# Two routing tables instead of four, filled by rows of 9,248 bytes, and the low half of w_out made by TensorE instead of GpSimd

## The chip, the core and the metric

The kernel runs on one core of a Trainium2 chip. The metric is the device time of one execution in microseconds, as a median over runs. The profile names the engines PE (TensorE, with PEld for its weight loads), DVE (VectorE), ACT (ScalarE), POOL (GpSimd) and SP (SyncE, which issues most DMAs; SPq and POOLq are the two issuing queues).

## What is computed

Eight batches of 576 tokens go through an attention with 32 packed keys (`_attn_ref`), a dense layer with a gate (`_moe_ref`), and a top-1 mixture of eight experts (`_moe2_ref`). Cut to what matters here:

```python
p_packed = sm_attn(p, k, v); out = sm_attn(q, p_packed, p_packed)   # 8 batches, 8 heads, 576 tokens, 64 wide
x = out as [4608, 512]
h = x @ w_in; g = h * sigmoid(h); x = g @ w_out                      # w_in [512, 2048], w_out [2048, 512]
e_idx = argmax(x @ w_gate)                                           # one of 8 experts per token
out[t] = gate[t] * eom[t] * (relu(x[t] @ w1[e]) @ w2[e])
```

## The kernel before

Everything is float32. TensorE multiplies at full rate in the rounded format float32r, so each factor is split into a high half (the value rounded to float32r) and a low half (value less high half), and each product is made of three matmuls: low by high, high by low, high by high.

The weights `w_in` and `w_out` come as 64-bit floats. `f64_load` (L432) brings a piece into a staging buffer, and `f64_conv` turns it into float32 on DVE with three instructions (L452, L455, L458). A piece of `w_in` goes straight into the tile `w_in`. A piece of `w_out` (128x512, 16 of them) goes into a tile `wf` (two buffers), and `split_out` then makes its two halves: `wo[0]`, the high one, by a cast on ACT (L469), and `wo[1]`, the low one, by a subtraction on POOL (L470).

All this happens while the first batch runs. A batch is a loop over 16 steps f. In a step PE makes `mm1(f)` (12 matmuls, L664) into the one buffer `ps_h`; ACT (L673) and DVE (L674) make `g` of it; ACT and DVE split it into `ghi` (L679) and `glo` (L684), and the 64 columns left over into `gl` (L691, and L693 on POOL in batch 0); PE makes `mm2(f-2)` (12 matmuls, L715). `mm1(f+1)` needs `ps_h` free, which is when `g(f)` is done. Into this loop are laid, by hand, the pieces of the attention of the next batch (`s1` to `s9`) and the products `step_m`. In batch 0 two or three pieces of the weights are converted in each step as well: one between `mm1` and `g`, one after `glo`. PE's small products share one PSUM buffer, the tag `a` (two of the eight banks; the others are the four accumulators and `ps_h`).

After step 4 of batch 0, `setup_late` fills the routing tables. Each token's place in its expert's list is found batch by batch; `place` (L782) scatters the token numbers into tables in DRAM by indirect DMAs from POOL. Block i goes to table i modulo NPERM (L35), so that scatters to one table, which have to wait for one another, stand four apart. Every slot must hold a default beforehand; the table that got no token adds nothing, and the sum over the tables is the token's row. `fetch_ix` reads the tables (L910, one DMA for each) and adds them up on POOL (L911, L912). The experts then run one block of 128 tokens after another.

The order on each engine is the order of the code. A DMA issued from SP waits in SP's queue until its buffer is free, and everything behind it waits too.

Of the kernel before, what the change touches and what calls it, by code (L numbers as in the profile page):

```python
# [8 lines left out]
F32 = mybir.dt.float32  # L9
F32R = mybir.dt.float32r  # L10
BF16 = mybir.dt.bfloat16
U32 = mybir.dt.uint32
I32 = mybir.dt.int32
ALU = mybir.AluOpType
AF = mybir.ActivationFunctionType
# [9 lines left out]
E8 = 8  # L25
F2 = 1024
NTOK = B * S
NBLK = NTOK // 128
CAP = NBLK
NPAIR = NBLK + E8 - 1  # L30
XW = DM + 1
# [3 lines left out]
HS = S // 2  # L35
EARLY = 3
NSTATIC = NBLK + 2
NPERM = 4
PW = 16


def constants():
    p = np.arange(128)
    c = np.zeros((128, C_END), np.float32)
    c[:, C_ID:C_ID + 128] = np.eye(128)
    e = np.arange(E8)
    c[:, C_E:C_E + E8] = e
    c[:, C_OFF:C_OFF + E8] = (e - E8) * CAP
    c[:, C_LT:C_LT + E8 * E8] = (e[None, :] < e[:, None]).reshape(1, -1)
    c[:, C_J] = p  # L50
    k = np.full((128, 256), 0x3F80, np.uint16)
    k[:, :128] *= p[:, None] < p[None, :]
    t = np.stack([block_tokens(i) for i in range(NBLK)], axis=1).astype(np.int32)
    t[:, np.arange(NBLK) % NPERM > 0] -= NTOK
    t = np.concatenate([t, np.zeros((128, PW - 1), np.int32)], axis=1)
    return {"cst": c, "cstk": k, "cstt": t}

# [17 lines left out]
def run(steps):  # L75
    now = list(steps)
    steps.clear()
    for st in now:
        st()


class Kernel:
    def __init__(self, tc, ins, out):
# [3 lines left out]
        self.ws2 = nc.dram_tensor("ws2", (E8, 4, 2, 128, 2 * DM), F32, kind="Internal").ap()  # L87
        self.perm = [nc.dram_tensor(f"perm{i}", ((E8 * CAP + 1) * 128, PW), I32, kind="Internal").ap() for i in range(NPERM)]
        self.xr = nc.dram_tensor("xr", (NTOK + 1, XW), F32, kind="Internal").ap()
# [5 lines left out]
    def run(self):  # L95
        tc, nc = self.tc, self.nc
# [20 lines left out]

        self.flip = False
        self.ppt, self.m, self.g, self.loads = {}, {}, {}, {}
        self.graws = []  # L120
        self.wgt = cp.tile([128, 4, E8], F32, name="wgt")
        self.tok = self.rt.tile([128, NBLK + PW - 1], I32, name="tok")
        self.w_in = self.pin.tile([128, 4, FF], F32, name="w_in")
# [42 lines left out]
    def setup_late(self):  # L166
        nc = self.nc
        nc.sync.dma_start(self.tri, self.i["cstk"].bitcast(BF16).rearrange("p (a b) -> p a b", a=2))
        nc.sync.dma_start(self.tok, self.i["cstt"])
        nc.gpsimd.memset(self.nt_run, 0.0)  # L170
        for i, perm in enumerate(self.perm):
            if i < 2:
                fill = self.stg.tile([128, E8 * CAP + 1], I32, tag="wf", bufs=2, name="fill")
                nc.gpsimd.memset(fill, 0 if i else NTOK)
            nc.sync.dma_start(perm.rearrange("(p c) w -> p (c w)", p=128).rearrange("p (w c) -> p w c", w=PW),
                              fill.unsqueeze(1).to_broadcast([128, PW, E8 * CAP + 1]))
        z = self.rt.tile([128, 5, XW], F32, tag="xr", name="zrow")[:1, 0]
        nc.gpsimd.memset(z, 0.0)
        nc.sync.dma_start(self.xr[NTOK:NTOK + 1, :], z)

    def pick(self):
        assert self.group is None and not self.late
# [90 lines left out]
    def prologue(self):  # L273
        nc = self.nc
# [55 lines left out]
        m_lo()  # L330
        att["s8", 1]()
        self.warm(24)
        att["s9", 0]()
        att["s9", 1]()
        self.gl = [self.p1.tile([128, NF, 128], F32R, tag=f"gl{i}", name="gl") for i in range(2)]

    def batch(self, b, hook=None):
        sched = self.extra_steps(b)
        for f in range(NF):
            s = b * NF + f  # L340
# [15 lines left out]
            self.fill(b, 2 if f < 2 else 1)  # L356
            if s > 1:
                self.mm2(*divmod(s - 2, NF))
            if slot and f == 1:
                self.split_slot()  # L360
            if wait and f == 1:
# [9 lines left out]
            if b == 0 and f == 0:  # L371
                t = self.rt.tile([128, 4, 512, 2], U32, tag="wg", name="stg4")
                for i in range(4):
                    self.f64_load(t[:, i], True)
            if b == 0 and f == 14:
                self.mid = self.rt.tile([128, E8 * DM], F32, tag="wg", name="mid")
                self.nc.sync.dma_start(self.wgt, self.i["wgt"])
            if b == 0 and f == 15:
# [88 lines left out]

    def split_out(self, w, f):
        self.nc.scalar.copy(out=self.wo[0][:, f, :], in_=w)  # L469
        self.nc.gpsimd.tensor_tensor(out=self.wo[1][:, f, :], in0=w, in1=self.wo[0][:, f, :].bitcast(F32), op=ALU.subtract)  # L470


    def split_store(self):
# [425 lines left out]
    def fetch_ix(self, j):  # L899
        nc = self.nc  # L900
        if j < EARLY:
            off = nc.values_load(self.ptab[0:1, 1 + j:2 + j], engines=[ENG.SP], min_val=0, max_val=E8 * CAP * 128)
            self.ex[j] = self.estar
        else:
            off = nc.values_load(self.tab[0:1, 0, j:j + 1], engines=[ENG.SP], min_val=0, max_val=E8 * CAP * 128)
            self.ex[j] = nc.values_load(self.tab[0:1, 1, j:j + 1], engines=[ENG.SP], min_val=0, max_val=E8 - 1)
        ix = self.rt.tile([128, NPERM + 2], I32, tag="xix_p", bufs=4, name="xix_p")
        at = self.rt.tile([128, 1], I32, tag="xix", bufs=6, name="xix")
        for i, perm in enumerate(self.perm):
            nc.sync.dma_start(ix[:, i:i + 1], perm[bass.ds(off, 128), 0:1])  # L910
        nc.gpsimd.tensor_tensor(out=ix[:, 4:6], in0=ix[:, 0:2], in1=ix[:, 2:4], op=ALU.add)  # L911
        nc.gpsimd.tensor_tensor(out=at, in0=ix[:, 4:5], in1=ix[:, 5:6], op=ALU.add)  # L912
        return at.bitcast(U32)

    def flag(self, j):
# [134 lines left out]
```

## Time and profile before

| | |
|---|---|
| time, median of 3 runs | 1361.1 us (1360.93 to 1362.29) |
| the profiled execution: its time, its span | 1360.51 us, 1358.7 us |
| PE busy | 1269.3 us, 93% |
| DVE, ACT, POOL busy | 653.9, 505.8, 173.4 us |
| batch 0: first and last `g` (L674) | 31.99 and 178.95 us |
| granted TensorE clock, mean | 0.971 of full speed |

The profile is of one execution. Times are counted from the start of its span. A busy PE is one whose matmuls are in flight; how fast they go depends on the granted clock, which has two levels, 1.2 GHz (shown as 0.50) and 2.4 GHz (1.00).

### The profile page before, as it was taken

The numbers are of one execution on the slowest core, as the hardware profiler recorded it, in microseconds if no ns is written. First come the engines' busy times: TensorE is split into PE (matmuls) and PEld (weight loads), VectorE is DVE, ScalarE is ACT, GpSimd is POOL, SyncE is SP. The second block draws the span as 40 slices with busy tenths as digits, with TensorE's granted clock in tenths as the row PEclk, the third lists the DMA queues.
The fourth block names the chain that finished last, engine by engine and source line by source line (L and its number), as shares of the span: only waits on it lengthen the run. The fifth ranks groups of instructions, "written<-read, shape, count | busy, mean of one in ns | idle before, by whom it ended". The sixth has DMA issues, their size and how long they took to land. (4 is left out here: it accounts for less than half of the span.)

```text
span 1358.7 us, 24463 instructions
## 1 busy us (share of the span) xinstructions
PE 1269.3 (93%) x8414; PEld 1020.1 (75%) x8416; DVE 653.9 (48%) x1417; ACT 505.8 (37%) x980; POOL 173.4 (13%) x236
## 2 busy tenths in 40 slices
PE   7754699999999899999999999999999999999997
PEld 3543578778788688787787788878888888888886
DVE  6953965845865745857556745232222222222221
ACT  3321255445464444454454433223223222222322
POOL 0220310100010100101000111112212212211210
PEclk9686899999999999999999999999999999999999
DMA  7598346846695855776665414442557383722630
GB/s 292 205 233 210 110 151 222 274 158 223 211 292 180 257 197 189 227 285 209 225 219 193 104 32 157 108 127 71 193 173 249 121 301 97 277 66 69 236 129 23
DMA packets 118303, 247.72 MB, mean 182 GB/s; under 512 B 30177, under 2 KB 56609, under 8 KB 118178
## 3 DMA queue, kind: packets, MB, share of 16 engines
q1 hardware_dynamic: 110946, 226.35, 51.0%
q0 software_dynamic: 7232, 19.72, 4.4%
q8 instruction: 77, 1.26, 0.4%
q14 instruction: 48, 0.39, 0.1%
HBM read 401.92 MB, written 96.29 MB: 367 GB/s over the span
## 5 line engine op out<-in xcount | busy, mean ns | idle before, releaser
L715 PE MATMUL acc<-wo,ghi 128*128 128x512 f32 x1024 | 320.9, 395 | 0.0
L715 PEld LDWEIGHTS acc<-wo,ghi 128*128 128x128 f32 x1024 | 194.5, 190 | 39.0
L664 PE MATMUL ps_h<-a,m_hi 128*128 128x288 f32 x1024 | 215.5, 303 | 0.8 <-DVE a L630 0.8
L715 PE MATMUL acc<-wo,glo 128*128 128x512 f32 x512 | 212.9, 416 | 0.0
L664 PE MATMUL ps_h<-a,m_lo 128*128 128x288 f32 x512 | 163.5, 319 | 30.9 <-DVE g L674 25.2
L1007 PE MATMUL py<-queue_q_buf,hhi 128*128 x608 | 190.7, 395 | 0.0
L979 PE MATMUL pu<-queue_q_buf,xhi 128*128 x560 | 174.6, 393 | 0.0
L664 PEld LDWEIGHTS ps_h<-a,m_hi 128*128 128x128 f32 x1024 | 171.1, 196 | 2.7 <-DVE a L630 1.0
L993 DVE TENSOR_TENSOR hlo<-ph,hhi 128x512 fp32r<-128x512 f32 x76 | 49.0, 686 | 247.3 <-ACT hhi L992 247.3
L674 DVE SCALAR_TENSOR_TENSOR g<-g,ps_h 128x576 f32<-128x576 f32 x128 | 96.1, 751 | 131.0 <-ACT g L673 130.2
L673 ACT ACTIVATE g<-ps_h 128x576 f32<-128x576 f32 x128 | 83.3, 651 | 188.8 <-PE ps_h L664 186.0
L664 PEld LDWEIGHTS ps_h<-a,m_lo 128*128 128x128 f32 x512 | 99.8, 195 | 57.0 <-DVE g L674 33.3
L1007 PEld LDWEIGHTS py<-queue_q_buf,hhi 128*128 128x128 f32 x608 | 114.5, 188 | 25.6
L715 PEld LDWEIGHTS acc<-wo,glo 128*128 128x128 f32 x512 | 97.3, 190 | 43.0 <-issue 24.8
L1007 PE MATMUL py<-queue_q_buf,hlo 128*128 x304 | 122.9, 404 | 0.0
L979 PEld LDWEIGHTS pu<-queue_q_buf,xhi 128*128 128x128 f32 x560 | 105.3, 188 | 22.4
L782 POOL DMA_INDIRECT perm<-tok,dsti x36 | 38.9, 1081 | 647.9 <-DVE dsti L779 507.4
L679 ACT CAST ghi<-g 128x512 fp32r<-128x512 f32 x128 | 79.4, 620 | 107.6 <-DVE g L674 106.5
L979 PE MATMUL pu<-queue_q_buf,xlo 128*128 x280 | 113.7, 406 | 0.3 <-ACT hs L981 0.3
L981 ACT ACTIVATE hs<-pu 128x512 f32<-128x512 f32 x76 | 45.4, 598 | 164.2 <-PE pu L979 162.5
L684 DVE TENSOR_TENSOR glo<-g,ghi 128x512 fp32r<-128x512 f32 x128 | 88.5, 692 | 31.1 <-ACT ghi L679 26.2
L1012 POOL DMA_INDIRECT out<-y,xix x38 | 38.2, 1006 | 328.2 <-ACT y L1010 320.6
(183 smaller groups left out, 1501.1 us busy)
## 6 DMA issues: line engine op xcount, KB each, us to landing
queue_q_buf<-ws SPq DMA_DIRECT2D x70, 4096.0 KB
ws<-shi SPq DMA_DIRECT2D x64, 512.0 KB
mid<-in_w SPq DMA_DIRECT2D x48, 512.0 KB
ws<-mid SPq DMA_DIRECT2D x48, 512.0 KB
att_v<-in_v SPq DMA_DIRECT2D x15, 640.0 KB
perm<-fill SPq DMA_DIRECT2D x4, 2312.0 KB
og<-in_wog SPq DMA_DIRECT2D x35, 256.0 KB
att_k<-in_k SPq DMA_DIRECT2D x15, 576.0 KB
```

The costliest lines, as they stand in the source:

```text
L664: nc.tensor.matmul(ps[:, hf, :288], lw[:, qd, fs], rx[:, qd, ts], start=(i == 0), stop=(i == 5))
L673: nc.scalar.activation(out=g2, in_=ps[:, :, :288], func=AF.Tanh, scale=0.5)
L674: nc.vector.scalar_tensor_tensor(out=g2, in0=g2, scalar=1.0, in1=ps[:, :, :288], op0=ALU.add, op1=ALU.mult)
L679: self.nc.scalar.copy(out=hi, in_=self.graw[:, :512])
L684: self.nc.vector.tensor_tensor(out=lo, in0=self.graw[:, :512], in1=self.ghi.bitcast(F32), op=ALU.subtract)
L715: self.nc.tensor.matmul(acc, l, r, start=(first and i == 0), stop=(last and i == 2))
L782: nc.gpsimd.indirect_dma_start(out=self.perm[(i0 + r) % NPERM], out_offset=bass.IndirectOffsetOnAxis(ap=di[:, r:r + 1], axis=0), in_=self. ...
L979: nc.tensor.matmul(ps, l[:, ks], w[:, k, r, ns], start=(i == 0), stop=(i == 11))
L981: nc.scalar.activation(out=self.hs[j][:, n * 512:n * 512 + 512], in_=ps, func=AF.Relu)
L993: nc.vector.tensor_tensor(out=lo[:, n], in0=ps, in1=hi[:, n].bitcast(F32), op=ALU.subtract)
L1007: nc.tensor.matmul(ps, l[:, k // 4, ks], w[:, k // 2, r, (k % 2) * DM:(k % 2) * DM + DM], start=(i == 0), stop=(i == 23))
L1012: nc.gpsimd.indirect_dma_start(out=self.out, out_offset=bass.IndirectOffsetOnAxis(ap=ix[:, 0:1], axis=0), in_=y, in_offset=None, bounds_ch ...
```

## The change

Two parts that have nothing to do with each other share the edit.

The tables: NPERM goes from 4 to 2, and the default becomes 2304 in both tables (the token numbers are lowered by the same). The source is one tile of 2,312 elements in each partition, written by one memset on POOL; each table is written by one DMA of 256 rows of 9,248 bytes, where four DMAs each wrote 2,048 rows of 1,156 bytes. The tile `fill` no longer takes the two buffers of `wf`; it takes the buffer of `xr`, which batch 0 does not use at that place. The row of zeros that ends `xr` is stored from the tile `zero` in the prologue. `fetch_ix` reads two tables and has one addition on POOL.

The low half of `w_out`: the subtraction on POOL goes. Later in the same step, after `mm2`, PE multiplies the identity (float32) by `wf` (float32), adds minus the identity (a new tile `neg`, float32r) times `wo[0]` into the same PSUM bank, and ACT casts the bank into `wo[1]`. The bank is of the shared tag `a`.

```diff
-NPERM = 4
+NPERM = 2
...
-    t[:, np.arange(NBLK) % NPERM > 0] -= NTOK
+    t -= NTOK // NPERM
...
     def setup_late(self):
...
-        for i, perm in enumerate(self.perm):
-            if i < 2:
-                fill = self.stg.tile([128, E8 * CAP + 1], I32, tag="wf", bufs=2, name="fill")
-                nc.gpsimd.memset(fill, 0 if i else NTOK)
-            nc.sync.dma_start(perm.rearrange("(p c) w -> p (c w)", p=128).rearrange("p (w c) -> p w c", w=PW),
-                              fill.unsqueeze(1).to_broadcast([128, PW, E8 * CAP + 1]))
-        z = self.rt.tile([128, 5, XW], F32, tag="xr", name="zrow")[:1, 0]
-        nc.gpsimd.memset(z, 0.0)
-        nc.sync.dma_start(self.xr[NTOK:NTOK + 1, :], z)
+        n = (E8 * CAP + 1) * PW // 2
+        fill = self.rt.tile([128, 5 * XW], I32, tag="xr", name="fill")[:, :n]
+        nc.gpsimd.memset(fill, NTOK // NPERM)
+        for perm in self.perm:
+            nc.sync.dma_start(perm.rearrange("(p c) w -> p (c w)", p=128).rearrange("p (h n) -> p h n", h=2),
+                              fill.unsqueeze(1).to_broadcast([128, 2, n]))
...
         self.warm(24)
+        nc.sync.dma_start(self.xr[NTOK:NTOK + 1, :].rearrange("o (p c) -> (o p) c", p=3), self.zero.bitcast(F32)[:3, :XW // 3])
...
                 self.mm2(*divmod(s - 2, NF))
+            if s:
+                run(self.wo_low)
...
+                self.neg = self.rt.tile([128, 256], F32R, tag="junk", bufs=1, name="neg")[:, :128]
+                self.nc.scalar.activation(out=self.neg, in_=self.ident, func=AF.Copy, scale=-1.0)
-            if b == 0 and f == 14:
+            if b == 0 and f == 15:
+                assert not self.f64_jobs and not self.f64_live and not self.wo_low
...
     def split_out(self, w, f):
         self.nc.scalar.copy(out=self.wo[0][:, f, :], in_=w)
-        self.nc.gpsimd.tensor_tensor(out=self.wo[1][:, f, :], in0=w, in1=self.wo[0][:, f, :].bitcast(F32), op=ALU.subtract)
+        self.wo_low.append(lambda: self.split_out_low(w, f))
+
+    def split_out_low(self, w, f):
+        nc = self.nc
+        ps = self.ps_a.tile([128, 2, 512], F32, tag="a", name="ps_w")
+        nc.tensor.matmul(ps[:, 0, :], self.ident, w, start=True, stop=False)
+        nc.tensor.matmul(ps[:, 0, :], self.neg, self.wo[0][:, f, :], start=False, stop=True)
+        nc.scalar.copy(out=self.wo[1][:, f, :], in_=ps[:, 0, :])
...
-        ix = self.rt.tile([128, NPERM + 2], I32, tag="xix_p", bufs=4, name="xix_p")
+        ix = self.rt.tile([128, NPERM], I32, tag="xix_p", bufs=4, name="xix_p")
...
-        nc.gpsimd.tensor_tensor(out=ix[:, 4:6], in0=ix[:, 0:2], in1=ix[:, 2:4], op=ALU.add)
-        nc.gpsimd.tensor_tensor(out=at, in0=ix[:, 4:5], in1=ix[:, 5:6], op=ALU.add)
+        nc.gpsimd.tensor_tensor(out=at, in0=ix[:, 0:1], in1=ix[:, 1:2], op=ALU.add)
```

SP's queue at `setup_late`, before: two constants, the four tables (`perm0` to `perm3`), the row of zeros, then the loads of the weights and `att_v`, the values for the attention of batch 1.

```order
L169 DMA tok_91<-in_cstt 128x51
L175 DMA perm0<-fill_654 2048x1x289
L175 DMA perm1<-fill_657 2048x1x289
L175 DMA perm2<-fill_657 2048x1x289
L175 DMA perm3<-fill_657 2048x1x289
L179 DMA xr<-zrow_662 1x513
L432 DMA stg4_401<-in_w_out 128x1024
L432 DMA stg4_401<-in_w_in 128x1024
L524 DMA att_v_732<-in_v 128x1280
```

The same place of SP's queue in the changed kernel:

```order
L169 DMA tok_91<-in_cstt 128x51
L175 DMA perm0<-fill_672 256x1x2312
L175 DMA perm1<-fill_672 256x1x2312
L435 DMA stg4_401<-in_w_out 128x1024
L435 DMA stg4_401<-in_w_in 128x1024
L534 DMA att_v_746<-in_v 128x1280
```

Three DMAs fewer stand ahead of the loads; nothing else has moved there.

On PE, step 4 of batch 0, before: the last two matmuls of `mm2(2)`, the transposes of attention step `s2` into the shared PSUM buffer, and the start of `mm1(5)`.

```order
L715 MATMUL acc3_493<-wo1_104,ghi_477 128x512
L715 MATMUL acc3_493<-wo0_103,ghi_477 128x512
L565 MATMUL ps_s_641<-cst_81,e1_396 128x128 x4
L565 MATMUL ps_s_641<-cst_81,e1_396 64x128
L664 MATMUL ps_h_665<-a2_95,m_lo_537 128x288
```

The same place in the changed kernel:

```order
L725 MATMUL acc3_501<-wo1_104,ghi_486 128x512
L725 MATMUL acc3_501<-wo0_103,ghi_486 128x512
L478 MATMUL ps_w_655<-wf_607,cst_81 128x512
L479 MATMUL ps_w_655<-wo0_103,neg_406 128x512
L575 MATMUL ps_s_659<-cst_81,e1_396 128x128 x4
L575 MATMUL ps_s_659<-cst_81,e1_396 64x128
L674 MATMUL ps_h_676<-a2_95,m_lo_549 128x288
```

Two matmuls into `ps_w` now stand between `mm2` and the attention step, and both share the PSUM buffer.

On ACT, step 11 of batch 0, where two pieces of `w_out` are converted in one step, in the changed kernel:

```order
L689 CAST ghi_1107<-g_1091 128x512
L701 CAST gl_351<-g_1091 128x64
L472 CAST wo0_103<-wf_1087 128x512
L472 CAST wo0_103<-wf_1114 128x512
L480 CAST wo1_104<-ps_w_1131 128x512
L480 CAST wo1_104<-ps_w_1135 128x512
L634 CAST a2_931<-y2_1139 128x2x288
```

Before, the two casts of `wo0` stood there alone; the two evacuations of `ps_w` now follow both, and the first of them so waits for the second piece's conversion.

## Rows read from the trace of the kernel before

**Rows 1.** Windows: busy time and count by engine, granted clock, DMA share, GB/s.
```profile
74.00:85.60 11.60, 0.15 (x12) 0.00 (x0) 2.44 (x4) 0.00 (x0) 0.00 (x0) 0.70 1.10 226
...
102.00:122.80 20.80, 1.17 (x40) 1.09 (x40) 1.43 (x2) 0.00 (x0) 0.20 (x1) 0.51 1.06 257
...
148.00:160.00 12.00, 8.97 (x56) 6.29 (x56) 11.64 (x17) 4.19 (x8) 5.82 (x5) 1.00 0.00 1
160.00:168.00 8.00, 5.41 (x33) 4.28 (x34) 7.81 (x11) 2.56 (x5) 3.91 (x4) 0.57 0.34 104
```
**Rows 2.** Window of all that follows batch 0 (columns as in rows 1).
```profile
183.00:1358.00 1175.00, 1151.37 (x7532) 936.01 (x7530) 528.69 (x1229) 453.77 (x875) 130.92 (x188) 1.00 0.54 179
```
**Rows 3.** Timeline, first standstill: start, duration, engine, operation [idle before, releaser].
```profile
68.99 23.88 SPq L175 DMA_DIRECT2D perm<-fill  x4
...
83.09 0.43 DVE L452 TENSOR_SCALAR wf<-stg 128x512 uint32<-128x512 uint32 x1 [13.17 <-DMA perm<-fill]
```
**Rows 4.** Timeline, second standstill.
```profile
121.63 1.30 PE L579 MATMUL ps_s<-att_v,a1t 128*32 128x64 f32 x40 [21.21 <-DMA att_v<-in_v]
...
122.99 0.28 DVE L581 TENSOR_SCALAR pp<-ps_s,sm 128x64 f32<-128x64 f32 x1 [19.52 <-PE ps_s L579]
```
**Rows 5.** Window of loads and stores with rows of 4 KB (columns as in rows 1).
```profile
191.00:192.00 1.00, 1.00 (x10) 1.00 (x8) 0.00 (x0) 1.00 (x3) 0.00 (x0) 1.00 1.05 430
```
**Rows 6.** Timeline: `g` of steps 0, 3, 10 and 14 of batch 0.
```profile
31.99 0.76 DVE L674 SCALAR_TENSOR_TENSOR g<-g,ps_h 128x576 f32<-128x576 f32 x1 [1.13 <-ACT g L673]
...
55.70 0.74 DVE L674 SCALAR_TENSOR_TENSOR g<-g,ps_h 128x576 f32<-128x576 f32 x1
...
141.89 0.74 DVE L674 SCALAR_TENSOR_TENSOR g<-g,ps_h 128x576 f32<-128x576 f32 x1
...
174.89 0.69 DVE L674 SCALAR_TENSOR_TENSOR g<-g,ps_h 128x576 f32<-128x576 f32 x1
```
**Rows 7.** Timeline: a subtraction on POOL, a conversion beside it, and one without it.
```profile
87.15 1.47 POOL L470 TENSOR_TENSOR wo<-wf,wo 128x512 fp32r<-128x512 f32 x1
...
87.51 1.66 DVE L455 SCALAR_TENSOR_TENSOR w_in<-stg,w_in 128x512 uint32<-128x512 uint32 x1
...
90.45 0.69 DVE L455 SCALAR_TENSOR_TENSOR wf<-stg,wf 128x512 uint32<-128x512 uint32 x1
```
**Rows 8.** Groups by form, 200 to 860 us, float32 matmuls: count, busy us, mean ns.
```profile
L535 PE MATMUL ps_m<-w_in,ppt 64*32 64x256 f32 x848 | 35.1, 388 | 0.0
...
L535 PE MATMUL ps_s<-att_k,att_p 64*32 64x288 f32 x176 | 7.9, 415 | 0.0
```
**Rows 9.** Timeline at full clock: first matmul of `mm1(9)`, of `mm2(7)`, of what follows.
```profile
129.65 0.38 PE L664 MATMUL ps_h<-a,m_lo 128*128 128x288 f32 x1
...
131.33 0.40 PE L715 MATMUL acc<-wo,glo 128*128 128x512 f32 x1
...
134.18 0.71 PE L535 MATMUL ps_s<-att_q,ppt 64*32 64x288 f32 x16
```
**Rows 10.** Timeline: the shared PSUM buffer handed from ACT to PE.
```profile
39.17 0.64 ACT L551 COPY e<-ps_s 128x576 f32<-128x576 f32 x1 [5.11 <-DVE sm L550]
...
39.87 1.11 PE L535 MATMUL ps_m<-w_in,ppt 64*32 64x256 f32 x16 [3.81 <-ACT e L551]
```
**Rows 11.** The scatters' landing; timeline of their last group, first read, first use.
```profile
DMA to landing us min/median/max: 4.7/6.2/9.5
...
869.23 0.96 POOL L782 DMA_INDIRECT perm<-tok,dsti  x1 [35.55 <-DVE dsti L779]
...
892.09 2.09 SPq L910 DMA_DIRECT2D xix_p<-perm  x4
...
900.15 0.63 PE L948 MATMUL px<-cst,x 128*128 128x128 f32 x4 [1.18 <-DVE hlo L993]
```
**Rows 12.** Timeline of POOL at `setup_late`.
```profile
68.62 0.62 POOL L174 MEMSET fill<- 128x289 int32 x2
...
86.51 0.68 POOL L693 TENSOR_TENSOR gl<-g,gl 128x64 fp32r<-128x64 f32 x1 [16.82 <-ACT gl L691]
```

More of the change, by code (lines that the diff above doesn't have):

```diff
@@ L119, in run @@
         self.ppt, self.m, self.g, self.loads = {}, {}, {}, {}
-        self.graws = []
+        self.graws, self.wo_low = [], []
         self.wgt = cp.tile([128, 4, E8], F32, name="wgt")
```

## Prediction

> **What bounds the kernel now.** I first read the windows of the whole span, to see where PE, the busiest engine, is not busy. After batch 0 there is nothing to win: from 183 us to the end PE is busy 1151.4 of 1175 us at full clock [rows 2]. So both halves of the change count by what they do to batch 0, which ends near 183 us, and to the hand-over to the experts.
>
> In batch 0 the windows show two standstills, and between them a DVE that is hardly ever free: 11.64 of 12 us against 8.97 for PE [rows 1]. The timeline says what the standstills are. The first: DVE waits 13.17 us for a buffer `wf` that the filling of the tables still reads; SP spends 23.88 us on issuing the four fills [rows 3]. The second: PE waits 21.21 us for the values `att_v`, whose load stands behind the fills, and DVE waits 19.52 us for PE's product [rows 4]. Counted on DVE, the engine that is otherwise full, the two cost 13.17 + 19.52 = 32.7 us. Meanwhile the DMA engines are saturated at 226 GB/s [rows 1], though rows of 4 KB go at 430 GB/s [rows 5].
>
> The rest of batch 0 is the distance between successive `g`: step 0 to step 14 takes 174.89 - 31.99 = 142.9 us, 110.2 without the standstills [rows 6].
>
> **The tables.** Four fills of 2,048 rows become two of 256 rows, 9.47 MB become 4.73 MB. First bound for the new time: the old rate, 4.73 MB at 226 GB/s, 20.9 us [rows 1]; second: the rate of 4 KB rows, 11.0 us [rows 5]. I take 12 us, since a row of 9,248 bytes is nearer to 4,096 than to 1,156. Issued near 70 us, the fills are then through at 82 us. The `wf` buffers are no longer taken, so the first wait goes. `att_v` is issued once the attention step of step 5 has read the old values, some 78 us, behind two loads of weights: 1.7 MB at 430 GB/s [rows 5] after 82 us is 86 us. It is needed at the end of step 7, three steps of some 7.5 us after 70 us, so at 92 us. Even with the slow bound it lands at 95 us. I take both standstills as gone: -32.7 us, with +3 for the slow bound.
>
> The Trainium skill ("DMA: Bandwidth & Descriptors", section "Why small descriptors are slow (HBM only)") says that a packet costs about 3 cycles on top of its 32-byte beats. That speaks against a gain by longer rows: at 1,156 bytes it is an estimated 8%, so the fills would take 19 us and the sum would come out some 2 us later. The trace does not agree: its two rates differ by 1.9 times.
>
> The memset that makes the source covers 2,312 elements where two of 289 took 0.62 us [rows 12], so 2.5 us (0.31 x 8) at most. POOL then waits 16.82 us for its next work [rows 12], and SP gets there only after a load that waits for DVE; without that cover it would cost the 2.5 us. The stored zero row, `neg` (one 128x128 pass on ACT) and the later `mid` are hidden by the half-idle ACT and SP; a fraction of a microsecond each if not.
>
> Reading two tables instead of four drops 76 small DMAs and 38 additions on POOL, beside a PE that is full [rows 2]: 0. Scatters to one table now stand two apart, so each third one waits for a landing, 4.7 to 9.5 us, median 6.2 [rows 11]. In batches 1 to 6 POOL has nothing else to do. In the last group, from 869.23 us, the third then goes at 875 us and lands at 882 us, and the scatter behind it at 882 us is not late: the first read is at 892.09 us [rows 11]. With landings of 9.5 us the read would come some 5 us late and PE's transposes at 900.15 us up to 4.6 us late [rows 11]. I take 0, upper end +4.6.
>
> **The low half of w_out.** On DVE it gives: a conversion that meets POOL's subtraction takes 1.66 us, one that does not 0.69 us [rows 7]. 16 pieces at 0.97 us are 15.5 us, worth that only while DVE sets the pace.
>
> On PE it costs. The trace has no float32 matmul of this shape. Its float32 products show two records for each instruction and 415 - 388 = 27 ns for 32 more columns, 0.84 ns a column [rows 8]; 512 columns twice are 0.86 us. The nearest float32r one has 12 in 2.85 us, 0.24 us [rows 9]. So a piece is 0.86 + 0.24 = 1.1 us at 2.4 GHz, twice that at 1.2 GHz; if the identity ran at the float32r pace it would be 0.5 us.
>
> Behind that comes a wait. `ps_w` uses the shared PSUM buffer, and the attention product behind it must wait until ACT has emptied it: 0.64 us and 0.06 us to restart [rows 10], 0.7 us, with `mm1` of the next step queued behind.
>
> I then walked the steps, each engine in its own order, with the durations of rows 3 and 6 to 10.
>
> - Steps 0 to 2, from 31.99 to 55.70 us [rows 6]: each loses 1 us of contention on DVE, but step 1 puts two pieces on PE at the low clock (2 x 2.2 us and a hand-over) ahead of `mm1(2)`, and step 2's piece waits for a conversion that comes after `g`. Together +0.7 us.
> - Steps 3 to 9, from 55.70 to 141.89 us [rows 6], 53.5 us without the standstills. PE now needs per step 1.68 for `mm1`, 2.85 for `mm2` [rows 9], 1.1 for its attention and `step_m` products (11 in 7 steps at 0.71 [rows 9]), 1.1 for the piece and 0.7 for the hand-over: 7.4 us, 52 in all. DVE without contention needs some 43. PE is the pace, and waits for ACT's cast of the high half add some 2 us: 53.8 us, +0.3.
> - Steps 10 to 13, 33.0 us before [rows 6]. Steps 11 and 12 have two pieces; ACT empties the first only after it has cast the second, whose conversion comes late, so PE stands 1.7 to 2.8 us in each. +2.7 us.
> - PE's lag of 1.8 us behind `g` at the end is then carried along, since from there PE is the bound.
> - Clock: PE's new waits will drop it now and then, as in rows 1 (0.57 in 160 to 168 us, after a stretch with gaps). I put 2 us on it.
>
> DVE's 15.5 us is thus spent: 0.7 + 0.3 + 2.7 + 1.8 + 2 = 7.5 us more in the steps. Sum: 1360.5 - 32.7 + 7.5 = 1335.3 us for the profiled execution, whose time is 0.6 us below the median; I forecast 1336 us.
>
> **The rivals.**
>
> - *DVE stays the pace.* If PE takes the pieces into its gaps (8.97 of 12 us busy in rows 1) or the identity is cheap, the 15.5 us come through too: 1360.5 - 32.7 - 15.5 = 1312 us. Against it: 7.4 us for PE per step, which leaves no gap. Half way, 1312 to 1324 us.
> - *The fills still block.* If long rows go no faster as a transfer than before, 41 us as in the trace (9.47 MB at 226 GB/s), `att_v` lands at 115 us in place of 92 us, and 22 us of the second standstill remain: 1358 us. For it: nothing in the trace has rows above 4 KB going to DRAM. Against it: rows 5. Partly so, 1348 to 1358 us.
> - *The clock stays low: slower than before.* At 1.2 GHz a step's PE work of 6.7 us doubles, so a step so run costs 6.7 us more. Of the steps 1 to 13, four at the low clock eat up the gain beyond 2 us, and from five on the kernel is slower: 1362 to 1375 us. For it: the clock fell to 0.51 to 0.57 where PE stood [rows 1], and the change puts a PE wait into every step. Against it: from 148 to 160 us PE is busy three quarters only and keeps 1.00 [rows 1]. The Trainium skill ("TensorE: Matmul & The Clock Gate", section "A second HAM failure mode: psum-queue depth-cycling") tells of a kernel whose short PE idles between groups, while it cycled through PSUM, made the clock swing between its two levels. By that rule this rival would hold; the 12 us at 1.00 do not agree.
>
> **How the numbers follow.** Forecast as summed (1325 to 1347 us) 0.72; DVE stays the pace 0.12; the fills still block 0.09; the clock stays low 0.07. The range leaves out the outer half of each rival: 1319 to 1350 us. About 0.2%, 2.7 us, is what a measurement here can tell from no change. Slower takes most of the clock rival, 0.04; same 0.03, from its edge and that of the fills; faster 0.93.
>
> **What would show it.** In the changed profile neither the wait of DVE for `fill` nor that of PE for `att_v` should be above 3 us; the fills should move at 300 GB/s or more. DVE's conversions should all take about 0.7 us. The identity's matmul should show two records and PE should go on some 1.1 us later; PE's idle time should be put down to ACT's casts of `wo` (L472, L480). The fifteenth `g` should come near 148 us. From there the two kernels should take equally long. The forecast is wrong if the clock is below 0.8 in most of batch 0, if a wait for a load remains, or if DVE is busier than PE between 75 and 140 us.

## The result, and the profile after

The changed kernel takes 1339.0 us (median of 4 runs, 1337.9 to 1340.3) against 1361.0 us before: a ratio of 0.984, 95% interval 0.982 to 0.986, or 22 us less. The forecast was 1336 us (1319 to 1350). The profiled execution, the slowest of the four, has 1340.3 us and a span of 1338.5 us, 20.2 us under the span of before (1358.7).

Windows of the changed kernel, with the columns of [rows 1]: two stretches of the fills and loads, two at the end of batch 0, and all that follows.

```profile
78.00:82.00 4.00, 3.33 (x52) 2.24 (x51) 3.25 (x7) 1.43 (x4) 0.68 (x1) 1.00 1.04 431
82.00:88.00 6.00, 5.32 (x28) 3.93 (x26) 4.79 (x8) 2.53 (x5) 0.68 (x1) 1.00 1.01 414
126.00:134.00 8.00, 5.53 (x17) 3.90 (x15) 3.85 (x7) 2.26 (x4) 1.42 (x1) 0.59 0.00 0
138.00:162.00 24.00, 20.56 (x142) 15.11 (x141) 11.57 (x21) 9.54 (x19) 4.64 (x5) 1.00 0.33 119
162.00:1337.00 1175.00, 1151.83 (x7533) 936.16 (x7532) 529.35 (x1229) 454.05 (x875) 123.39 (x150) 1.00 0.53 179
```

The transfers move at 414 to 431 GB/s where they moved at 226 [rows 1]. The last row answers to [rows 2]: after batch 0 PE is as busy as it was. The whole difference lies ahead of 162 us. The third row is the one place in the second half of batch 0 where the clock falls; in the first half it is low in places up to 62 us.

Timeline of SP's queue in the changed kernel, which answers to [rows 3]:

```profile
76.20 1.29 SPq L175 DMA_DIRECT2D perm<-fill  x2
77.58 1.28 SPq L435 DMA_DIRECT2D stg<-in_w_out  x1
80.84 0.33 SPq L435 DMA_DIRECT2D stg<-in_w_in  x1
81.27 1.19 SPq L534 DMA_DIRECT2D att_v<-in_v  x1
```

Groups of PE and DVE in the changed kernel, 28 to 165 us (count, busy us, mean ns, idle time ahead and what ended it):

```profile
L589 PE MATMUL ps_s<-att_v,a1t 128*32 128x64 f32 x80 | 1.5, 221 | 2.3 <-DMA att_v<-in_v 1.6 <-ACT wo L480 0.7
...
L684 DVE SCALAR_TENSOR_TENSOR g<-g,ps_h 128x576 f32<-128x576 f32 x17 | 12.8, 752 | 21.9 <-ACT g L683 21.9
L458 DVE SCALAR_TENSOR_TENSOR wf<-stg,wf 128x512 uint32<-128x512 uint32 x16 | 11.9, 746 | 0.6
L461 DVE SCALAR_TENSOR_TENSOR wf<-stg,wf 128x512 uint32<-128x512 uint32 x16 | 11.1, 692 | 0.5
```

Issuing the fills holds SP for 1.29 us in place of 23.88, DVE has no wait for `fill`, and the 21.21 us of [rows 4] are 1.6. The conversions' instructions with two inputs take 0.69 us, all but one: the 746 ns of L458 are a mean, with 1.54 us at 121.31 us, beside a POOL operation with two inputs (shown at the end). In return DVE, which outside the standstills waited 4.3 us for `g` in all of batch 0, now waits 21.9 us for it, that is for PE. PE has become the pace. Steps 3 to 9 as one window (columns of [rows 1]), and one of PE's waits in it (timeline):

```profile
60.52:114.55 54.03, 48.03 (x368) 34.96 (x368) 42.74 (x71) 23.71 (x49) 6.79 (x9) 1.00 0.68 246
```

```profile
65.07 0.72 PE L545 MATMUL ps_s<-att_k,att_p 64*32 64x288 f32 x16 [0.68 <-ACT wo L480]
```

PE is busy 48.0 of 54.0 us. The other 6.0 us are six hand-overs of the shared PSUM buffer like the one shown (4.1 us), the 1.6 us for `att_v` and 0.4 us for a cast.

Timeline of the changed kernel: `g` of steps 0, 2, 3, 10 and 14 of batch 0, to hold against [rows 6].

```profile
33.37 0.75 DVE L684 SCALAR_TENSOR_TENSOR g<-g,ps_h 128x576 f32<-128x576 f32 x1 [1.13 <-ACT g L683]
...
51.05 0.75 DVE L684 SCALAR_TENSOR_TENSOR g<-g,ps_h 128x576 f32<-128x576 f32 x1 [2.78 <-ACT g L683]
...
60.52 0.76 DVE L684 SCALAR_TENSOR_TENSOR g<-g,ps_h 128x576 f32<-128x576 f32 x1 [3.62 <-ACT g L683]
...
114.55 0.75 DVE L684 SCALAR_TENSOR_TENSOR g<-g,ps_h 128x576 f32<-128x576 f32 x1
...
152.53 0.75 DVE L684 SCALAR_TENSOR_TENSOR g<-g,ps_h 128x576 f32<-128x576 f32 x1 [1.67 <-ACT g L683]
```

Such starts of `g` give the length of each stage. The table has it for every kernel that ran, from the profiled execution of each; the last stage ends with the first `g` of batch 1. Times are medians, in us; the kernels are told of below. Beside these runs the kernel before took 1360.0 to 1362.0 us, and each ratio below is to the time beside it; times that lie less than some 2 us apart do not tell which kernel is faster.

| kernel | time | steps 0-2 | 3-9 | 10-13 | 14-15 |
|---|---|---|---|---|---|
| before | 1361.0 | 23.7 | 86.2 | 33.0 | 7.8 |
| changed | 1339.0 | 27.2 | 54.0 | 38.0 | 9.4 |
| tables alone | 1328.5 | 23.7 | 55.0 | 33.1 | 7.9 |
| low half alone | 1371.1 | 27.1 | 87.2 | 37.0 | 9.4 |
| two tables, short rows | 1350.9 | 26.3 | 67.9 | 36.9 | 9.5 |
| four tables, long rows | 1352.0 | 26.4 | 68.1 | 37.9 | 9.4 |
| identity in float32r | 1334.3 | 24.0 | 52.9 | 36.4 | 9.4 |
| pieces inside `mm2` | 1337.4 | 23.8 | 50.1 | 41.0 | 9.4 |
| ... with late fills | 1335.5 | 23.5 | 48.7 | 41.4 | 9.4 |
| subtraction on DVE | 1326.1 | 23.1 | 52.2 | 32.0 | 9.4 |
| ... with late fills | 1323.9 | 23.1 | 49.7 | 32.0 | 9.4 |
| no low half | 1320.1 | 20.6 | 52.5 | 29.0 | 8.5 |
| ... with late fills | 1314.4 | 20.6 | 43.8 | 29.0 | 8.5 |
| split PE and DVE, late fills | 1321.5 | 23.1 | 48.3 | 32.6 | 7.9 |

The first `g` comes between 31.1 and 33.5 us in these fourteen executions, 33.4 us in the changed kernel's and 31.5 us with the tables alone, which has the same code ahead of it. So the 1.4 us that the changed kernel's profile starts later than that of before are taken as scatter, not as a cost of the change.

### The profile page after: what moved, and what is told of

The parts are those of the page before. It is cut to its first block, busy times and chain, and to the rows that moved or that the text cites. A ratio compares the mean times of both kernels' runs of the same rounds, so it can differ in the third digit from the quotient of the medians.

```text
span 1338.5 us, 24244 instructions
## 1 busy us (share of the span) xinstructions
PE 1282.2 (96%) x8462; PEld 1023.7 (76%) x8464; DVE 640.2 (48%) x1417; ACT 515.7 (39%) x997; POOL 143.8 (11%) x180
## 3 DMA queue, kind: packets, MB, share of 16 engines
q1 hardware_dynamic: 92294, 221.57, 48.3%
## 5 line engine op out<-in xcount | busy, mean ns | idle before, releaser
L674 PE MATMUL ps_h<-a,m_hi 128*128 128x288 f32 x1024 | 211.4, 299 | 0.6 <-DVE a L640 0.6
L674 PEld LDWEIGHTS ps_h<-a,m_hi 128*128 128x128 f32 x1024 | 167.8, 192 | 3.0 <-DVE a L640 0.9
L725 PEld LDWEIGHTS acc<-wo,glo 128*128 128x128 f32 x512 | 96.1, 188 | 42.3 <-issue 24.3
L694 DVE TENSOR_TENSOR glo<-g,ghi 128x512 fp32r<-128x512 f32 x128 | 88.5, 692 | 31.1 <-ACT ghi L689 26.2
L494 DVE TENSOR_TENSOR mid<-mid,shi 128x1024 fp32r<-128x1024 f32 x48 | 58.8, 1226 | 43.2 <-ACT shi L493 43.2
```

Source lines behind the costliest of these rows:

```text
L494: nc.vector.tensor_tensor(out=w.bitcast(F32R), in0=w, in1=hi.bitcast(F32), op=ALU.subtract)
L674: nc.tensor.matmul(ps[:, hf, :288], lw[:, qd, fs], rx[:, qd, ts], start=(i == 0), stop=(i == 5))
L694: self.nc.vector.tensor_tensor(out=lo, in0=self.graw[:, :512], in1=self.ghi.bitcast(F32), op=ALU.subtract)
L725: self.nc.tensor.matmul(acc, l, r, start=(first and i == 0), stop=(last and i == 2))
```

## The experiments

**Each half alone.** The tables alone: the changed kernel with POOL's subtraction back in `split_out`, and without `neg`.

```diff
...
-        self.wo_low.append(lambda: self.split_out_low(w, f))
+        self.nc.gpsimd.tensor_tensor(out=self.wo[1][:, f, :], in0=w, in1=self.wo[0][:, f, :].bitcast(F32), op=ALU.subtract)
```

> The two tables with long rows alone; the low half of w_out is again POOL's subtraction, as before. Theory (the tables give all of the gain, 32.7 us of standstill, and the low half on TensorE costs 7.5 to 12 us net, since PE becomes the pace of batch 0): 1360.5 - 32.7 = 1328 us, 8 to 13 us under the changed kernel's 1339, DVE conversions again up to 1.66 us, and the g of steps 10 to 14 as far apart as before (33.0 us). Rival (the low half pays too, because it frees DVE of the contention with POOL): 1345 to 1355 us, more than the changed kernel takes.

Measured: 1328.5 us, ratio to before 0.977 (0.975 to 0.978), 31.5 us less. Steps 3 to 9 lose 31.2 us; the other stages are those of before. The low half alone puts `split_out_low` and `neg` into the kernel before:

> The low half on TensorE alone; four tables with short rows, as before. Theory: both standstills stay (13 and 21 us) and PE's additional work costs 7.5 to 12 us in the steps around them, part of which the standstills take up: 1361 to 1373 us, not faster than before. Rival (the low half pays, 15.5 us of DVE time): 1345 to 1352 us. The first g also tells whether the start (33.4 us in the changed kernel, 32.0 before) goes with the place of the zero row's store, which here is as before: 32.0 if so.

Measured: 1371.1 us, ratio 1.009 (1.007 to 1.010). Both standstills stay, as its waits show (total us, times, longest):

```profile
PE ps_s L591 <- DMA att_v<-in_v: 16.7, 1, 16.7
DVE wf L457 <- DMA perm<-fill: 15.8, 1, 15.8
```

So the change is two changes of opposite sign: the tables give 31.5 us, and the low half on PE costs 10 to 11 us, alone and with the tables alike (1371.1 - 1360.0, both on one chip, and 1339.0 - 1328.5, on two chips). The rival, that the freed DVE pays for it, falls. The first `g` of the low half alone comes at 31.1 us, with the zero row's store where it was; that of the tables alone, where the store is moved, comes at 31.5 us. So the place of the store is not seen to set the start.

**What of the tables counts: bytes or rows.** Two tables, each again filled by 2,048 rows of 1,156 bytes:

```diff
-            nc.sync.dma_start(perm.rearrange("(p c) w -> p (c w)", p=128).rearrange("p (h n) -> p h n", h=2),
-                              fill.unsqueeze(1).to_broadcast([128, 2, n]))
+            nc.sync.dma_start(perm.rearrange("(p c) w -> p (c w)", p=128).rearrange("p (w c) -> p w c", w=PW),
+                              fill[:, :E8 * CAP + 1].unsqueeze(1).to_broadcast([128, PW, E8 * CAP + 1]))
```

> As the changed kernel, but each of its two tables is filled by 2,048 rows of 1,156 bytes, as before, in place of 256 rows of 9,248: the same 4.73 MB. Theory (short rows are what slowed the transfer): at the 226 GB/s of before the fills take 21 us in place of 11, the load of att_v behind them lands some 10 us later, and of these PE, which now waits 1.6 us for it, waits nearly all: 1346 to 1350 us. Rival (the fills' bytes and number decided, not the row's length; two fills of half the rows no longer hold up SP's queue): 1338 to 1342 us.

And four tables with long rows (NPERM = 4, with the sums over four in `fetch_ix` and the constants to match):

> As the changed kernel, but with four tables, each filled by long rows: 9.47 MB. Theory (at 420 to 440 GB/s they take 22 us in place of 11, so that att_v lands some 11 us later; the queue of SP is not held up, so DVE's wait for the fill stays away): 1347 to 1351 us, the wait of PE for att_v at 10 to 13 us. Rival (long rows alone give the gain, since the blocked queue was what cost): 1338 to 1342 us.

Measured: 1350.9 and 1352.0 us, ratios 0.993 (0.991 to 0.995) and 0.994 (0.992 to 0.996). Both theories hold, 1 us beyond their ranges. Short rows: timeline of SP's queue, then a window of the transfers, then a wait of PE (total us, times, longest).

```profile
73.58 3.54 SPq L175 DMA_DIRECT2D perm<-fill  x2
77.22 10.54 SPq L435 DMA_DIRECT2D stg<-in_w_out  x1
```

```profile
82.00:88.00 6.00, 5.32 (x42) 3.67 (x42) 4.26 (x7) 3.21 (x8) 0.68 (x1) 1.00 1.10 227
```

```profile
PE ps_s L589 <- DMA att_v<-in_v: 13.1, 1, 13.1
```

The same three for long rows and four tables:

```profile
73.97 4.03 SPq L175 DMA_DIRECT2D perm<-fill  x4
```

```profile
82.00:88.00 6.00, 5.32 (x43) 3.80 (x41) 4.56 (x8) 2.88 (x7) 0.68 (x1) 1.00 1.02 422
```

```profile
PE ps_s L589 <- DMA att_v<-in_v: 12.9, 1, 12.9
```

Half the bytes at 227 GB/s and all of them at 422 GB/s take about equally long, and PE's wait for `att_v` is 13 us in both. Each of the two measures is worth 12 to 13 us when the other is there already. What one of them is worth by itself is not shown: both kernels are 19 to 20 us faster than the low half alone (1371.1), but both also keep a third part of the change, the tile `fill` outside the two buffers of `wf`, which no run takes alone. The starts of `g` say where those 19 to 20 us lie. From `g` 4 to `g` 5, over the first standstill, it is 22.3 us with the low half alone and 8.0 us in both kernels: with either measure DVE no longer waits for `fill`, and the freed buffers may be all that this needed. From `g` 7 to `g` 8, over the second standstill, it is 25.2 us with the low half alone, 22.2 us with short rows, 22.0 us with four tables, and 8.8 us in the changed kernel: this one goes only with both measures.

**What of the low half costs.** First the product: the identity cast to float32r (a new tile `pos`), times the cast high half, so that its low half is zero.

```diff
...
-        nc.tensor.matmul(ps[:, 0, :], self.ident, w, start=True, stop=False)
+        nc.tensor.matmul(ps[:, 0, :], self.pos, self.wo[0][:, f, :], start=True, stop=False)
```

> As the changed kernel, but the identity's product is a float32r one with the cast high half (as the second product has), so that the low half comes out as zero; the rest is the same, hand-over too. A piece should take 0.5 us on PE in place of 1.1 (2.4 GHz). Theory (PE's time sets the pace of batch 0): 16 x 0.6 = 10 us less, 1329 to 1332 us. Rival (the waits around a piece, for ACT's cast ahead of it and for ACT's emptying behind it, set the pace, not its columns): 1335 to 1339 us.

Measured: 1334.3 us, ratio 0.981 (0.979 to 0.982), 4.7 us less than the changed kernel: between the two theories. Steps 0 to 2 win 3.2 us, steps 3 to 13 together 2.7. Part of what is missing to the 10 us is due to the edit: the first product, too, now waits for ACT's cast (7.5 us, where only the second product did, 3.2 us).

Then the place. A piece stands between the second and the third block of `mm2` and, where `w_out` comes once a step, one step later:

```diff
...
+            if j == 1:
+                self.low(1 if self.f64_live else 0)
...
+            if s > 1:
+                self.low(1, self.f64_live[:1] and self.f64_live[0][0][0] == "out")
             self.fill(b, 2 if f < 2 else 1)
...
-            if s:
+            if s == 1:
                 run(self.wo_low)
...
+    def low(self, keep, when=True):
+        while when and len(self.wo_low) > keep:
+            self.wo_low.pop(0)()
```

> As the changed kernel, but a piece is queued on PE between the second and the third of the four blocks of mm2, and one step later where w_out comes once a step: its conversion and cast are then done, and the emptying by ACT lies under the other two blocks. In the steps with two pieces (11 to 13) the second goes ahead of the next step's mm2. The products are the same. Theory (of a piece's 1.1 + 0.7 us the 0.7 and most of the waits for casts go, some 11 + 4 us): 1339 - 15 = 1322 to 1328 us, with the wait for att_v, 5.8 us where the steps run fastest, as the next bound. Rival (the time of the products alone costs, wherever they stand): 1335 to 1339 us.

Measured: 1337.4 us, ratio 0.983 (0.981 to 0.985), within its interval no different from the changed kernel. In the sum the theory falls and the time is that of the rival, but the stages show another reason. Steps 0 to 2 win 3.4 us and steps 3 to 9 win 3.9, though the products are the same: the waits did cost. Steps 10 to 13 lose 3.0. (The profiled execution, at 1335.5 us, is the fastest of four, which reach to 1340.6; so the stages win more than the medians.) There the second piece of a step now stands right behind `step_m`, in the shared PSUM buffer, which DVE empties only when its queue comes to it. Waits of this kernel, 105 to 147 us:

```profile
DVE g L690 <- ACT g L689: 8.1, 2, 6.0
...
PE ps_w L484 <- DVE m_lo L662: 6.0, 2, 4.4
```

**The bound without the low half.** A cast of `w_out` by ACT takes its place:

```diff
     def split_out_low(self, w, f):
...
-        nc.tensor.matmul(ps[:, 0, :], self.ident, w, start=True, stop=False)
-        nc.tensor.matmul(ps[:, 0, :], self.neg, self.wo[0][:, f, :], start=False, stop=True)
-        nc.scalar.copy(out=self.wo[1][:, f, :], in_=ps[:, 0, :])
+        self.nc.scalar.copy(out=self.wo[1][:, f, :], in_=w)
```

> As the changed kernel, but without the low half: its place in w_out's second buffer gets a cast of w_out by ACT, so that part of the computation is left out, and POOL, PE and DVE have nothing to do for it. Theory: the pace is that of DVE without contention, 1360.5 - 32.7 - 15.5 = 1312 us, 27 us under the changed kernel; so much the low half on PE costs in all. Rival (PE and the loads bound batch 0 without the pieces too): 1325 us or more, and the pieces cost at most 14 us.

Measured: 1320.1 us, ratio 0.970 (0.968 to 0.971), between the theories. The faster steps arrive at the next wait, the one for `att_v`, which had grown from 1.6 to 5.8 us, and PE restarts at half clock (timeline, then a window):

```profile
87.66 1.30 PE L583 MATMUL ps_s<-att_v,a1t 128*32 128x64 f32 x40 [5.76 <-DMA att_v<-in_v]
```

```profile
86.00:92.00 6.00, 4.34 (x52) 3.99 (x52) 2.00 (x4) 0.00 (x0) 0.00 (x0) 0.50 0.83 338
```

With the fills queued behind step 7, so behind `att_v`:

```diff
-            if b == 0 and f == 4:
+            if b == 0 and f == 7:
                 self.setup_late()
```

> As the kernel without the low half (that part of the computation is left out; its place gets a cast of w_out), but with the fills behind step 7. Theory (it took 1320 us and not the 1312 of the sum because PE waits 5.8 us for att_v and restarts at the low clock): 1320 - 6 = 1312 to 1315 us. Rival (something other than att_v keeps it at 1320): 1318 us or more.

Measured: 1314.4 us, ratio 0.965 (0.964 to 0.966). PE starts that product at 80.45 us, without a wait:

```profile
80.45 0.77 PE L583 MATMUL ps_s<-att_v,a1t 128*32 128x64 f32 x40
```

**Better versions.** The subtraction goes to DVE, at the start of the next step, when the cast is done:

```diff
...
+            run(self.wo_low)
             self.fill(b, 1, True)
...
     def split_out_low(self, w, f):
...
+        self.nc.vector.tensor_tensor(out=self.wo[1][:, f, :], in0=w, in1=self.wo[0][:, f, :].bitcast(F32), op=ALU.subtract)
```

> The two tables with long rows, and the low half as a subtraction on DVE at the start of the next step. 16 subtractions of 128x512 at the 0.69 us that glo takes are 11 us of DVE time, without any contention with POOL (16 x 0.97 = 15.5 us given back) and without a piece or a hand-over on PE. Theory (DVE without contention has time to spare, PE's pieces are what the changed kernel waits for): 1360.5 - 32.7 - 15.5 + 11 = 1323 us, about 16 us under the changed kernel and some 5 under the tables alone. Rival (DVE's length is the pace of batch 0 in every form, and the subtractions come ahead of g in its queue): 1335 us or more.

Measured: 1326.1 us, ratio 0.975 (0.973 to 0.976). The subtractions take 0.67 us each. Against the tables alone it is 2.4 us, half of what was expected, and the intervals overlap. With the fills behind step 7:

> As the kernel with the subtraction on DVE (1326 us), but the two fills are queued behind step 7 in place of step 4, that is behind the load of att_v in place of ahead of it. Theory (4.73 MB at 420 GB/s put 11 us ahead of att_v, for which PE there waits 4.4 us and then restarts at the low clock; behind step 7 the transfer engines are idle three quarters of the time): step 8 shrinks from 10.6 to about 7 us, 1321 to 1323 us. Rival (the loads of w_out are then what is late, DVE waits for stg in steps 8 to 11): 1325 us or more.

Measured: 1323.9 us, ratio 0.972 (0.970 to 0.974); the wait for `att_v` is gone, and the way from `g` 7 to `g` 8 shrinks from 10.6 to 8.6 us, not to the 7 of the theory. The rival's wait for `stg` is not there. What is there is the memset for the fills, which came with them into this step, where DVE has no gap (timelines of DVE and POOL):

```profile
84.71 2.56 DVE L452 TENSOR_SCALAR w_in<-stg 128x512 uint32<-128x512 uint32 x1
...
84.95 2.03 POOL L173 MEMSET fill<- 128x2312 int32 x1
```

The DVE operation takes 0.55 us in the same step with early fills, so the memset costs some 2.0 us there; the last section has more on this. The pieces inside `mm2` with late fills:

> As the kernel with the pieces inside mm2, and with the fills behind step 7 in place of step 4. Theory (what is left then is DVE's pace with PE's pieces hidden): 3 to 5 us under the kernel with the pieces inside mm2, 1318 to 1324 us. Rival (PE's 6.7 to 7 us a step stay the pace, so that att_v isn't waited for and the fills' place is worth nothing): the same time as with the fills behind step 4.

Measured: 1335.5 us, ratio 0.981 (0.979 to 0.982), 1.9 us less than with early fills, which the two intervals do not tell from none: the rival holds. By the table, the steps with two pieces (10 to 13, 41.4 us), not `att_v`, are what that kernel loses by. The last version takes from each the stages in which it is best:

```diff
...
-        self.wo_low.append(lambda: self.split_out_low(w, f))
+        if 2 < f < 11:
+            self.wo_low.append(lambda: self.split_out_low(w, f))
+        else:
+            self.wo_dve.append(lambda: self.nc.vector.tensor_tensor(
+                out=self.wo[1][:, f, :], in0=w, in1=self.wo[0][:, f, :].bitcast(F32), op=ALU.subtract))
...
```

> The low half split between two engines, with the fills behind step 7: the eight pieces of w_out that come once a step (3 to 10) on PE inside mm2, as in the kernel with the pieces there, and the eight that come in twos (0 to 2 and 11 to 15) as DVE subtractions at the start of the next step. Theory (from the two traces: steps 3 to 9 take 48.7 us with the pieces inside mm2 and 49.7 with the subtraction; steps 0 to 2 and 10 to 13 take 23.1 and 32.0 us with the subtraction and 23.5 and 41.4 with the pieces): 1 us under the subtraction throughout, 1321 to 1324 us. Rival (in steps 0 to 9 the pace is DVE's either way and the change of place costs a wait): 1324 us or more.

Measured: 1321.5 us, ratio 0.970 (0.969 to 0.972), 17.5 us below the changed kernel and, by the medians, the fastest that leaves nothing out (1323.9 us is next, and the two intervals overlap). In steps 3 to 9 its pieces stand between blocks of `mm2` with hardly a wait; the last of the eight, in step 11, stands behind `step_m` and waits 4.38 us (timeline of PE):

```profile
62.88 1.13 PE L488 MATMUL ps_w<-wf,cst 128*128 128x512 f32 x2 [0.52 <-DVE m_lo L666]
63.44 0.79 PE L489 MATMUL ps_w<-wo,neg 128*128 128x512 f32 x1
64.07 0.39 PE L737 MATMUL acc<-wo,glo 128*128 128x512 f32 x1
...
113.29 2.07 PE L488 MATMUL ps_w<-wf,cst 128*128 128x512 f32 x2 [4.38 <-DVE m_lo L666]
```

## Why the prediction was right, and where it was off

**The tables, -32.7 us: right.** Alone they give 31.5 us, and 31.2 us of it in the stage of the standstills. What is missing of the 32.7 is less than the wait for `att_v` that they still have, 2.7 us. The fills move at more than 410 GB/s. The rival that they still block falls, but with little to spare, and in part by luck. The forecast had the fills issued near 70 us and `att_v` landed at 86 us, at the latest at 95. In the changed kernel SP issues them at 76.20 us, `att_v` lands at 96.1 us, and PE waits only 1.6 us because the steps, too, come later: it wants `att_v` at 94.5 us where the forecast had 92. As soon as the steps get faster, the wait grows, to 5.8 us without the low half.

**Steps 0 to 2, +0.7 us: the step that was mis-sized.** They take 3.4 us more: step 0 is 1.1 us shorter, step 1 is 1.8 us longer and step 2 is 2.8 us longer. Pieces and waits of PE there (timeline of the changed kernel):

```profile
42.73 2.07 PE L478 MATMUL ps_w<-wf,cst 128*128 128x512 f32 x2 [1.46 <-DVE m_lo L656]
...
45.90 2.07 PE L478 MATMUL ps_w<-wf,cst 128*128 128x512 f32 x2 [0.68 <-ACT wo L480]
...
48.20 0.44 PE L674 MATMUL ps_h<-a,m_lo 128*128 128x288 f32 x1
...
55.24 1.59 PE L478 MATMUL ps_w<-wf,cst 128*128 128x512 f32 x2 [2.22 <-DVE wf L461]
...
57.05 0.44 PE L674 MATMUL ps_h<-a,m_lo 128*128 128x288 f32 x1
```

The two pieces of step 1 take 48.20 - 42.73 = 5.5 us, near the 5.1 that the forecast had. So what it priced too low is step 2, as far as can be told: it gave the three steps one sum. The piece of step 2 waits for a conversion that follows `g` on DVE, and `mm1(3)`, on which the next `g` waits, follows the piece on PE. So DVE's part, the piece (1.8 us at the fallen clock) and `mm1` (2.6 us) come one after the other, and DVE stands 3.62 us. From `g` 2 to `g` 3 it is 9.5 us, 2.8 more than before, as much as the error of 2.7. With the piece put off by a step it is 5.8 us (timelines of DVE: `g` 2 of before, whose `g` 3 is in [rows 6], then both with the pieces inside `mm2`):

```profile
48.98 0.74 DVE L674 SCALAR_TENSOR_TENSOR g<-g,ps_h 128x576 f32<-128x576 f32 x1
```

```profile
49.64 0.75 DVE L690 SCALAR_TENSOR_TENSOR g<-g,ps_h 128x576 f32<-128x576 f32 x1 [3.13 <-ACT g L689]
...
55.40 0.75 DVE L690 SCALAR_TENSOR_TENSOR g<-g,ps_h 128x576 f32<-128x576 f32 x1
```

Not all of it is the chain: at full clock the piece takes 1.2 us and `mm1` 1.7, as `mm1` did in this step before, so some 1.5 of the 2.8 us are the clock.

**Steps 3 to 9, +0.3 us: right.** They take 54.0 us where 53.8 was forecast. PE's work is 48.0 us (forecast 47), the hand-overs 4.1 (forecast 4.9). The 2 us put on waits for casts are only 0.4, and the 1.6 us for `att_v`, put at nothing, stand in their place; that the sum fits so closely is luck. A piece takes 1.1 to 1.2 us on PE, as estimated, and its records come in twos. The 43 us that were put on DVE alone are 43.8 us in the kernel without the low half and with late fills.

**Steps 10 to 13, +2.7 us and 2 us for the clock: right.** Together +5.0 us. Here, too, the rows show it (timeline of PE in steps 11 and 12):

```profile
128.73 2.07 PE L478 MATMUL ps_w<-wf,cst 128*128 128x512 f32 x2 [2.47 <-ACT wo L480]
...
131.03 0.44 PE L674 MATMUL ps_h<-a,m_lo 128*128 128x288 f32 x1
...
140.14 1.12 PE L478 MATMUL ps_w<-wf,cst 128*128 128x512 f32 x2 [1.35 <-ACT wo L480]
...
142.16 0.72 PE L545 MATMUL ps_s<-att_q,ppt 64*32 64x288 f32 x16 [0.67 <-ACT wo L480]
```

The second pieces wait 2.47 and 1.35 us, because ACT empties the first only after the second's cast; the hand-over behind is 0.67 us. After the long wait of step 11 the clock is 0.59 (126 to 134 us): the piece up to `mm1` takes 2.3 us where the later one takes 1.35, and `mm1` 3.0 us (131.03 to 134.04) where it takes 1.7 us in step 12 (142.81 to 144.51). That is 2.3 us for the clock. The forecast put its 2 us on no step; with the 1.5 us of step 2 the clock costs nearer 3.8. Nor is a low clock new here: over steps 10 to 13 its mean was 0.84 before and is 0.91 now. Before, it cost little, because DVE was the pace: in the step with the lowest clock (0.64, 161.19 to 169.85 us) DVE was busy 8.40 of 8.66 us. Without the low half, steps 10 to 13 take 29.0 us at a mean clock of 1.00 (early fills) and at 0.82 (late fills) alike.

**The lag of PE, 1.8 us: right in size,** 1.6 us (steps 14 and 15, 9.4 against 7.8 us). But the kernels with the subtraction on DVE, with no piece on PE, have the same 9.4 us, so the pieces are not its cause; what is stays open. After that both kernels take equally long: from the first `g` of batch 1, at 161.97 us and before at 182.73 us, to the end of the span it is 1176.5 and 1176.0 us.

**DVE's gain, 15.5 us: too high.** The conversions' instructions with two inputs take 52.2 us in all with the tables alone and 40.6 us in the changed kernel: 11.6 us of contention. It entered the sum only as something spent.

**The rivals.** *DVE stays the pace* (1312 us) did not happen. The kernel without the low half comes near its price, at 1314.4 us, but only with the fills moved, of which the rival knew nothing; with the fills where the change has them it takes 1320.1 us. *The clock stays low* did not happen either: from 66 us on it is 0.59 for one stretch, and 1.00 from 66 to 122 us and from 138 us on. The Trainium skill's rule ("TensorE: Matmul & The Clock Gate", section "A second HAM failure mode: psum-queue depth-cycling") has the clock swing where PE idles between groups; by the trace it fell at the two waits of step 11 (1.34 and 2.47 us), and stayed at 1.00 at those of step 12 (1.35 and 0.67 us) and at the hand-overs of steps 3 to 9 (0.68 us each).

**The signs.** The fifteenth `g`, forecast near 148 us, came at 152.53 us. The other signs came as forecast, but for the one conversion of 1.54 us: between 75 and 140 us PE is busy 54.3 us and DVE 47.7.

So of the 5.0 us by which the profiled execution came out above the sum (1340.3 against 1335.3), 2.7 are those of steps 0 to 2, 1.4 the later start of this one execution, and the rest is spread.

## What to carry to other kernels

Measure the parts of a change apart: here a gain of 31 us carried a loss of 10 with it, and inside the gain a moved buffer stayed untested beside the bytes and the rows. Moving work off a contended engine pays only if the engine that takes it has gaps where the work fits; a product that waits for a conversion of its own step ties the two engines in series, and put off by a step, between blocks that need none of its buffers, the same product costs half (3.2 against 6.5 us in steps 0 to 2, over the kernel without the low half). When a wait is taken away, look for the next transfer behind it: queueing the fills behind the load that is needed first gave 6 us more without the low half, and some 2 us, hardly clear of noise, in two other kernels.

## What was not expected of the hardware

Row length counts as much as bytes: 256-row fills went at 414 to 431 GB/s, 2,048-row fills at 227, and behind two of the latter the next issue of SP took 10.54 us.

POOL's memset of 2.02 us holds up one kind of DVE operation and not another. In the changed kernel (timelines of DVE and POOL) a TENSOR_SCALAR that elsewhere takes 0.42 to 0.55 us ends only after it:

```profile
70.79 2.55 DVE L455 TENSOR_SCALAR w_in<-stg 128x512 uint32<-128x512 uint32 x1
...
71.04 2.02 POOL L173 MEMSET fill<- 128x2312 int32 x1
```

With the subtraction on DVE the two met in the same way, but there the TENSOR_SCALAR kept its length and the memset took 0.26 us longer. The operations with two inputs behind it run beside the memset at their usual length:

```profile
64.50 0.55 DVE L452 TENSOR_SCALAR w_in<-stg 128x512 uint32<-128x512 uint32 x1
...
64.74 2.28 POOL L173 MEMSET fill<- 128x2312 int32 x1
...
65.08 0.70 DVE L455 SCALAR_TENSOR_TENSOR w_in<-stg,w_in 128x512 uint32<-128x512 uint32 x1
```

Beside a POOL operation with two inputs they do not. This is the one long conversion of the changed kernel:

```profile
121.14 1.16 POOL L629 TENSOR_TENSOR x<-x,mx 128x576 f32<-128x576 f32 x1 [3.05 <-DVE mx L627]
...
121.31 1.54 DVE L458 SCALAR_TENSOR_TENSOR wf<-stg,wf 128x512 uint32<-128x512 uint32 x1
```

The Trainium skill ("SBUF — State Buffer", section "SBUF: two separate sides") says that DVE and GpSimd hold one port pair by turns, and that a DVE operation with two inputs there is blocked only by a GpSimd operation that reads. The rows agree: beside the memset, which only writes, 0.70 us; beside POOL operations that read, 1.54 us here and 1.66 us in [rows 7].
